# Pooled values of the first batch summed in two chains of transfers and an addition

## The chip, the cores and the metric

The kernel runs on one core of a Trainium2 chip. The metric is the device time of one execution in microseconds. The core's engines take their instructions in program order, each engine from a queue of its own: PE (matmul), DVE (vector), ACT (scalar), POOL, and SP, which here only starts transfers. Engines wait for one another through semaphores; transfers run on 16 shared DMA engines.

## The reference

Attention with two parts that are added, then two feed-forward layers over all 2304 tokens:

```python
# q, k, v: (4 batches, 8 heads, 576 tokens, 64)
q_d, k_d, v_d = mean over groups of 4 tokens          # 144 pooled tokens
out_up = repeat(softmax(q_d k_d^T / 8) v_d, 4)        # each pooled row four times
out_local = softmax(q k^T / 8 where |i - j| < 4) v
x = (out_up + out_local) as (2304, 512)
x = relu(x @ w_in1)**2 @ w_out1                       # w_in1 512x2048, w_out1 2048x512
out = silu(x @ w_in2) @ w_out2                        # a second pair of weights
```

## The kernel before

A list scheduler in Python writes the program. Every step of the work is a coroutine that yields the engine it wants next with an estimated cost; the step that can start earliest by these estimates comes next, and ties are broken by a rank: ten times the place at which it was added, plus an entry of the table SHIFT. What the scheduler decides is fixed when the program is built. On the chip each engine runs its list in order and stalls where its next instruction has to wait.

**Batch 0, the start.** `load_pooled(0)` brings the pooled values of batch 0: the input holds the four members of each group of tokens as four arrays of 72 x 1024 f32 (288 KB), and four transfers issued by POOL (line 412) write the first into the tile `vd_t` (called dst in the traces) and add the other three to it on the way. `pooled(0, hp)`, for the four pairs of heads, sums q and k on DVE (L458) and copies them by PE and ACT (L465, L467), makes scores (L475), the maximum (L479), the exponential (L486), the normalised weights (L492), transposes them (L498, L500) and multiplies them with `vd_t` (L510); ACT takes the result out (L513). The first L510 is the first reader of `vd_t`.

Between these stand eight tiles of 72 tokens of the local attention, `tile_attention(i)`: scores (L586, L589), maximum (L599), exponential (ACT alone, L604, four times, where the tile is in the tuple ATILE; otherwise DVE L608, ACT L611, DVE L614), normalisation on DVE (L268, L616, L617), transposes (L626), copy (L629), product (L638) and copy out (L645). `tiles_done` adds the pooled part to the local one (L890), four head pairs for each half of the batch. `keep_warm` gives PE small products (L1540) where the scheduler expects a gap.

**Weights.** They lie in memory as 8-byte words. `eighth(m, e)` loads 1 MB (SP, L304) into one of three raw buffers and rebuilds 128 x 1024 f32 from it by ACT (L312) and DVE (L268, L271). Here w_in e and w_out e are eighth e of the first pair. They take the buffers in turn (w_in 0, w_out 0, w_in 1, w_out 1, ...), so that a load waits on SP until the eighth three places before it is rebuilt. A later step, `quarter`, squares and sums them (L333, L341, PE L344 and L354).

**The first layer.** The first two chunks of 128 hidden units (L1027, 16 products in two halves of the tokens) need the finished x of batch 0 and w_in 0. The next chunks (L1049, f32) need w_in 1 and so on, the second product is L1106, and from the second stretch of tokens on the products are f16 (L1062, L1106). PE then goes through products with few breaks to the end.

**Batch 1** loads q and k as a whole (SP, L550, L551), sums them on POOL (L432, L434) and goes on to L475. The second pair's w_out is loaded through the tile `gr`, after x2d of the first layer has been read back.

Of the kernel before, what the change touches and what calls it, by code (L numbers as in the profile page):

```python
# [13 lines left out]
ALU = mybir.AluOpType  # L14
# [4 lines left out]
NT, DM, DFF = 2304, 512, 2048  # L19
# [11 lines left out]
HG = NG // 2  # L31
# [10 lines left out]
EXP_MASK = 0x7F800000  # L42
SLACK = 1.02

PADS = (0.4, 0.4, 1.2, 0.4)

ATILE = (0, 2, 3, 4, 5, 14, 15)

FILL = 0.2

SHIFT = {('eighth', 'i2', 0): -185,
 ('eighth', 'i2', 1): -185,
 ('eighth', 'i2', 2): -185,
 ('eighth', 'i2', 3): -185,
 ('eighth', 'i2', 4): -225,
 ('eighth', 'i2', 5): -225,
# [4 lines left out]
 ('load_v', 8): 94,  # L61
 ('load_v', 12): 35,
 ('load_v', 14): 105,
 ('load_v0', 1): -22,
 ('piece', 3, 1, 0): 337,
 ('pooled', 0, 3): 51,
 ('pooled', 3, 3): -81,
 ('products', 10): 1,
 ('quarter', 'i1', 0): -152,
 ('quarter', 'i1', 1): -152,  # L70
 ('quarter', 'i1', 2): -152,
# [3 lines left out]
 ('quarter', 'o1', 3): -77,  # L75
 ('quarter', 'o2', 0): 15,
 ('split_late', 4, 2): 321,
 ('tile_attention', 2): 53,
 ('tile_attention', 3): 72,
 ('tile_attention', 11): 32,  # L80
 ('unit', 8): 52,
 ('unit', 9): -135,
 ('unit', 10): -57}

N1 = 3

# [8 lines left out]
class Schedule:  # L95
# [15 lines left out]
    def mark(self, key):  # L111
        self.events[key] = self.end
# [62 lines left out]
def tile_attention_two_moes(ctx: ExitStack, tc: tile.TileContext, qw, kw, vw, qt, kt, vt, qp, kp, vp, maskd, tmaskd,  # L175
# [7 lines left out]
    V, A, G, PE = nc.vector, nc.scalar, nc.gpsimd, nc.tensor  # L183
# [16 lines left out]
    gr = pool.tile([P, 7 * 512], F32, name="gr")  # L200
# [191 lines left out]
    def raw_buf(at, n=2048):  # L392
        return words(int(at), n).bitcast(U32)
# [4 lines left out]
    vd_t = dst[0:HG, 4 * NGP + 4 * NG:].rearrange("p (c n) -> p c n", c=2)  # L398
# [6 lines left out]
    def load_pooled(b):  # L405
        yield "DVE", 0.1
        V.memset(qd_t[:, :, NG:], 0.0)
        if b == 0:
            for r in range(4):
                yield "POOL", 1.1  # L410
                yield "DMA", 0.82, 2.0
                G.dma_start(out=vd_t, in_=vp[0, r], **({"accum_op": ALU.add} if r else {}))
        else:
            for r in range(4):
                kw_ = {"accum_op": ALU.add} if r else {}
                if b > 1:
                    yield "POOL", 2.1
                    G.dma_start(out=qd_t[:, :, :NG], in_=qp[b - 2, r], **kw_)
                    G.dma_start(out=kd_t, in_=kp[b - 2, r], **kw_)
                yield "POOL", 1.1  # L420
                yield "DMA", 1.5 if b == 1 else 4.5, 2.0
                G.dma_start(out=vd_t, in_=vp[b, r], **kw_)
        outd[b] = p2.tile([P, 4, NG], F32, tag="outd", name="outd")
        mark(("pooled", b))
# [12 lines left out]
    def pooled(b, hp, banks):  # L437
        pad = PADS[b]
        if b > 1:
# [124 lines left out]
    def tile_attention(i, banks):  # L564
# [27 lines left out]
        if i >= 2:  # L592
            yield "event", ("tr", i - 2)
        by_act = i in ATILE
        yield "DVE", 0.48 if by_act else 0.85
# [951 lines left out]
    with tc.manual_schedule():  # L1547
# [40 lines left out]
        for h in range(4):  # L1588
            add(load_qk(0, h))
        add(load_pooled(0))  # L1590
        convert(0)
        for h in range(2):
# [7 lines left out]
        for n in range(1, 16):  # L1600
            convert(n, *([("qk", 0, 3)] if n == 1 else [("at", 3)] if n < 4 else []))
            if n == 3:
                add(split_early(0))
            if n == N1:
                add(load_pooled(1), ("xf", 0))
                for h in range(2):
                    add(load_qk(1, h), ("xf", 0))
                for hp in range(4):
                    add(sums(1, hp), ("xf", 0))
                for hp in range(4):  # L1610
                    add(pooled(1, hp, TWO))
                add(all_pooled(1))
                for i in range(per, 2 * per):
                    add(tile_attention(i, TWO), ("xf", 0))
                add(tiles_done(1))
            if n % 4 == 3 and n >= NFULL:
                add(quarter("i1", n // 4), ("xf", 0))
                add(quarter("o1", n // 4), ("xf", 0))
                add(first_scales(0, 1, n // 4))
# [4 lines left out]
        add(whole("o1"))  # L1624
        add(split_early(1))
        add(load_pooled(2), ("ds", 1), ("at", TPB - 1))
        for hp in range(4):
            add(pooled(2, hp, TWO))
# [14 lines left out]
        r = [[raw_buf(a * 1024)] for a in (22, 26, 28)]  # L1643
# [4 lines left out]
        r = [[gr[:, 1536 + i * 1024:2560 + i * 1024].bitcast(U32) for i in range(2)], [raw_buf(31 * 1024)]]  # L1648
# [122 lines left out]
```

## Time and profile before

| | |
|---|---|
| median of three runs | 882.69 us (879.0, 882.69, 884.89) |
| the profiled execution | 884.28 us, of which the span of the trace is 882.3 |
| PE busy | 851.1 us, 96% of the span |
| DVE, ACT, POOL busy | 673.6, 524.6, 59.7 us |
| granted clock of PE, mean | 0.991 of full speed |

The span runs from the first to the last instruction of the trace; 2.0 us of the execution's time lie outside it. PE is the engine that is nearly always busy, so what counts is where PE waits, or works at a lower clock.

### The profile page before, as it was taken

How to read it: one execution, taken by the hardware profiler on the slowest of the kernel's cores; microseconds unless marked ns; L12 is line 12 of the kernel's file. 1: busy time of each engine (PE TensorE's matmuls, PEld its weight loads, DVE VectorE, ACT ScalarE, POOL GpSimd, SP SyncE). 2: the span in 40 equal slices, each digit the busy share in tenths (PEclk: the TensorE clock that was granted, in tenths of full speed). 3: DMA queues.
4: the chain of work that ended last, by engine and by line, in shares of the span. 5: the costliest groups of instructions: out<-in, count | busy, mean ns of one | idle time of the engine just before them, and what ended most of it. 6: DMA issues, size and time to landing. Idle time of an engine off the chain costs nothing.

```text
span 882.3 us, 14418 instructions
## 1 busy us (share of the span) xinstructions
PE 851.1 (96%) x5578; PEld 507.6 (58%) x5578; DVE 673.6 (76%) x1310; ACT 524.6 (59%) x1026; POOL 59.7 (7%) x86
## 2 busy tenths in 40 slices
PE   8898999999988999999999999999999899999998
PEld 6664554455433444444444445884445778788865
DVE  5567888886667999888988998746988887777731
ACT  3787888888767652435665443666676564344432
POOL 1016113000000400000000000000000110000000
PEclk9899999999999999999999999999999999999999
DMA  9678456844667951242124200322333200010010
GB/s 253 206 200 321 172 157 147 238 164 160 225 201 250 229 135 37 89 155 72 36 84 155 72 28 27 114 61 96 132 113 107 81 25 2 25 49 1 2 48 25
DMA packets 35584, 103.55 MB, mean 117 GB/s; under 512 B 4316, under 2 KB 8540, under 8 KB 32316
## 3 DMA queue, kind: packets, MB, share of 16 engines
q1 hardware_dynamic: 27036, 84.65, 29.0%
q0 software_dynamic: 8192, 17.83, 8.4%
q8 instruction: 44, 0.72, 0.3%
q14 instruction: 24, 0.20, 0.1%
q10 hardware_dynamic: 288, 0.15, 0.1%
HBM read 82.16 MB, written 20.45 MB: 116 GB/s over the span
## 4 chain that ended last, share of the span: by engine, by line
PE 71%; DMA 11%; DVE 8%; ACT 7%; issue 2%; POOL 1%; SPq 0%; POOLq 0%; DVEq 0%; ACTq 0%
PE acc L1106 26%; PE hps L1062 24%; PE seven L1181 6%; PE acc L1216 4%; DMA dst<-vp 4%; DMA wt<-w_in 3%; DMA gr<-w_out 3%; PE hps L1049 2%; DVE ub L1242 1%; DVE gr L271 1%; PE pb L1216 1%; DVE wt L271 1%; ACT sq L333 1%; PE hps L1027 1%; DVE hl L271 1%
## 5 line engine op out<-in xcount | busy, mean ns | idle before, releaser
L1062 PE MATMUL hps<-hl,wt 128*128 128x512 f16 (+1 forms) x1440 | 293.7, 351 | 0.0
L1062 PEld LDWEIGHTS <-wt 128*128 128x128 f16 x1440 | 140.2, 98 | 128.4 <-issue 3.6
L1106 PE MATMUL acc<-gr,wt 128*128 128x512 f16 (+2 forms) x928 | 212.8, 374 | 0.0
L1106 PEld LDWEIGHTS <-wt 128*128 128x128 f16 x864 | 84.5, 99 | 78.3 <-issue 1.2
L271 DVE SCALAR_TENSOR_TENSOR gr<-hps,sc,gr 128x512 f16<-128x512 f32 (+1 forms) x118 | 80.2, 679 | 63.2 <-ACT gr L1476 60.4
L1106 PE MATMUL acc<-wt,gr 128*128 128x512 f16 x480 | 112.0, 379 | 0.1
L1458 ACT ACTIVATE hps<-hps,sc 128x512 f32<-128x512 f32 (+1 forms) x72 | 44.0, 611 | 90.5 <-PE hps L1062 90.2
L1181 PE MATMUL seven<-hl,wt 128*128 128x256 f16 x456 | 80.5, 275 | 5.7 <-DVE ub L1242 5.6
L1473 ACT ACTIVATE hps<-hps,sc 128x512 f32<-128x512 f32 (+1 forms) x46 | 27.4, 596 | 91.5 <-PE hps L1062 87.6
L1106 PEld LDWEIGHTS <-gr 128*128 128x128 f16 x480 | 46.8, 98 | 51.8 <-issue 0.7
L1181 PEld LDWEIGHTS <-wt 128*128 128x128 f16 x672 | 66.1, 98 | 17.9 <-issue 7.5
L1476 ACT ACTIVATE gr<-hps,sc 128x512 f16<-128x512 f32 (+1 forms) x118 | 74.3, 630 | 2.7
L1216 PEld LDWEIGHTS <-gr 128*128 128x128 f16 x672 | 65.6, 98 | 11.0 <-DVE gr L271 2.0
L1216 PE MATMUL acc<-wt,gr 128*128 128x256 f16 x480 | 61.0, 274 | 2.2 <-DVE gr L271 1.1
L1181 PE MATMUL seven<-ub,wt 128*128 128x256 f16 x180 | 49.6, 275 | 0.0
L1242 DVE TENSOR_TENSOR ub<-seven,ub 128x256 f32<-128x256 f32 x74 | 28.6, 419 | 21.8 <-PE seven L1181 20.0
L271 DVE SCALAR_TENSOR_TENSOR wt<-wt,sc 128x1024 f16<-128x1024 f32 x32 | 40.6, 1279 | 4.7 <-ACT wt L372 4.4
L778 DVE TENSOR_REDUCE ub<-ub 128x128 f32<-128x896 f32 x40 | 43.3, 1083 | 1.0
L711 DVE TENSOR_TENSOR ub<-ub,s 128x896 f32<-128x896 f32 x40 | 43.5, 1087 | 0.6
L746 DVE TENSOR_REDUCE s<-ub 128x14 f32<-128x896 f32 x40 | 43.2, 1080 | 0.5
L708 DVE TENSOR_TENSOR ub<-ub 128x896 f32<-128x896 f32 x40 | 43.2, 1081 | 0.0
L271 DVE SCALAR_TENSOR_TENSOR gr<-ub,sc,gr 128x512 f16<-128x512 f32 (+2 forms) x66 | 42.1, 671 | 0.7 <-ACT gr L1476 0.7
(247 smaller groups left out, 1159.1 us busy)
## 6 DMA issues: line engine op xcount, KB each, us to landing
wt<-w_in SPq DMA_DIRECT2D x16, 1024.0 KB, 8.2
wt<-w_out SPq DMA_DIRECT2D x9, 1024.0 KB, 5.5
w<-wt POOLq DMA_DIRECT2D x16, 512.0 KB, 4.6
dst<-w SPq DMA_DIRECT2D x16, 512.0 KB, 3.3
gr<-w_out SPq DMA_DIRECT2D x14, 512.0 KB, 5.4
ub<-vw SPq DMA_DIRECT2D x10, 640.0 KB, 3.8
ub<-kw SPq DMA_DIRECT2D x10, 640.0 KB, 7.2
dst<-vp POOLq DMA_DIRECT2D x16, 288.0 KB, 6.9
```

The costliest lines, as they stand in the source:

```text
L271: V.scalar_tensor_tensor(out=out, in0=in0, scalar=s, in1=in1, op0=op0, op1=op1)
L708: eng.tensor_tensor(out=prod[i % 2].rearrange("p (t w d) -> p t w d", t=2, w=WIN), in0=band(k, j, t0), in1=q[:, j, t0:t0 + 2, :].unsqueeze ...
L711: eng.tensor_tensor(out=prod[i % 2].rearrange("p (t d w) -> p t d w", t=2, d=D), in0=band_v(v, j, t0), in1=prob[u][:, j, t0:t0 + 2, :].uns ...
L746: V.tensor_reduce(out=s[:, j, t0:t0 + 2, :], in_=prod[i % 2].rearrange("p (t w d) -> p t w d", t=2, w=WIN), axis=AX.X, op=ALU.add)
L778: V.tensor_reduce(out=o[:, t0:t0 + 2, j, :], in_=prod[i % 2].rearrange("p (t d w) -> p t d w", t=2, d=D), axis=AX.X, op=ALU.add)
L1062: PE.matmul(out=ps, lhsT=w[:, o:o + P], rhs=x[:, kk, :n], start=(m == 0), stop=(m == 3 * KD - 1))
L1106: PE.matmul(out=a, lhsT=l, rhs=x, start=(first and m == 0), stop=(last and m == len(ops) - 1))
L1181: PE.matmul(out=b7[:, i * 256:(i + 1) * 256], lhsT=a[:, c:c + P], rhs=x, start=(n == 0), stop=(n == 5))
L1216: PE.matmul(out=acc7[p][m][:, t, :], lhsT=a, rhs=b, start=(e == 0 and t == 0 and n == 0), stop=(e == 7 and t == 1 and n == 2))
L1242: V.tensor_tensor(out=out, in0=a, in1=b, op=op)
L1458: A.activation(out=ps, in_=ps, func=AF.Relu, scale=1.0 if exact else cs)
L1476: A.activation(out=gh, in_=ps, func=AF.Copy, scale=sg)
```

## The change

`load_pooled(0)` writes the first and the second array by plain transfers into two tiles, `vd_t` and `vo_t` (a part of `gr`, not in use at that time), adds the third to `vd_t` and the fourth to `vo_t`, and then adds the two tiles by one DVE instruction (L426, 72 x 1024 f32). The scheduler's table of ranks, the tuple ATILE of tiles whose exponential is made by ACT alone, and one entry of PADS (batch 2) are other ones. Line numbers after the change are 11 to 14 higher.

```diff
-PADS = (0.4, 0.4, 1.2, 0.4)
+PADS = (0.4, 0.4, 0.8, 0.4)
-ATILE = (0, 2, 3, 4, 5, 14, 15)
+ATILE = (0, 1, 2, 5, 9, 10, 14, 15)
 SHIFT = {('eighth', 'i2', 0): -185,
...
- ('eighth', 'i2', 2): -185,
...
- ('load_v0', 1): -22,
- ('piece', 3, 1, 0): 337,
+ ('piece', 3, 1, 0): 456,
...
+ ('pooled', 2, 0): -10,
+ ('pooled', 3, 0): 148,
...
+ ('sum_weights', 'o2', 4): 26,
...
- ('unit', 10): -57}
+ ('unit', 10): 108,
+ ('unit', 16): 18}
...
         if b == 0:
-            for r in range(4):
+            vo_t = gr[0:HG, 0:2 * DM].rearrange("p (c n) -> p c n", c=2)
+            for r, t in enumerate((vd_t, vo_t, vd_t, vo_t)):
                 yield "POOL", 1.1
-                yield "DMA", 0.82, 2.0
-                G.dma_start(out=vd_t, in_=vp[0, r], **({"accum_op": ALU.add} if r else {}))
+                yield "DMA", 0.82, 2.0 if r == 3 else 2.0
+                G.dma_start(out=t, in_=vp[0, r], **({"accum_op": ALU.add} if r > 1 else {}))
+            yield "DVE", 1.1
+            V.tensor_tensor(out=vd_t, in0=vd_t, in1=vo_t, op=ALU.add)
```

SP's list at the start, behind the eight loads of q and k of batch 0. First before (L560 loads the values of four tiles, L576 those of one; L304 the weights, w_in and w_out in turn):

```order
L560 DMA wt<-vt 70x4x512
L304 DMA wt<-w_in 128x2048
L560 DMA wt<-vt 70x4x512
L304 DMA wt<-w_out 128x2048
L304 DMA wt<-w_in 128x2048 x2
L304 DMA wt<-w_out 128x2048 x2
L576 DMA wt<-vt 70x512
L304 DMA wt<-w_out 128x2048
L304 DMA wt<-w_in 128x2048 x2
L550 DMA ub<-qt 128x1152
```

and after:

```order
L315 DMA wt<-w_in 128x2048
L574 DMA wt<-vt 70x4x512 x2
L315 DMA wt<-w_out 128x2048
L315 DMA wt<-w_in 128x2048
L315 DMA wt<-w_out 128x2048
L315 DMA wt<-w_in 128x2048
L315 DMA wt<-w_out 128x2048
L315 DMA wt<-w_in 128x2048
L590 DMA wt<-vt 70x512
L315 DMA wt<-w_out 128x2048
L315 DMA wt<-w_in 128x2048 x2
L315 DMA wt<-w_out 128x2048
```

Before, w_in 0, w_out 0, w_in 2, w_in 1, w_out 1 and w_out 3 stand there in this order; after, w_in 0, w_out 0, w_in 2, w_out 3, w_in 1, w_out 1, w_in 5. The load of w_out 3, which waits until w_in 2 is rebuilt, has moved ahead of those of w_in 1 and w_out 1, and the loads of q and k of batch 1 (L550, L564 after) stand further back.

DVE's list around the rebuilding of w_out 0 (the row wt<-wt of L268 and that of L271), before:

```order
L479 TENSOR_REDUCE dmx<-acc_369 128x3
L268 TENSOR_SCALAR dmx<-dmx 128x3
L268 TENSOR_SCALAR wt<-wt 128x1024
L271 SCALAR_TENSOR_TENSOR wt<-wt 128x1024
L268 TENSOR_SCALAR asm<-asm 128x4
L616 RECIPROCAL asm<-asm 128x4
L617 TENSOR_TENSOR ae<-ae,asm 128x280
L268 TENSOR_SCALAR dsm<-dsm 128x3
L491 RECIPROCAL dsm<-dsm 128x3
L492 TENSOR_TENSOR hl_71<-hl_71,dsm 128x432
```

and after (L279 and L282 are the L268 and L271 of before):

```order
L493 TENSOR_REDUCE dmx<-acc_391 128x3
L279 TENSOR_SCALAR dmx<-dmx 128x3
L279 TENSOR_SCALAR wt<-wt 128x1024
L628 TENSOR_REDUCE asm<-ae 128x4
L279 TENSOR_SCALAR asm<-asm 128x4
L630 RECIPROCAL asm<-asm 128x4
L631 TENSOR_TENSOR ae<-ae,asm 128x280
L282 SCALAR_TENSOR_TENSOR wt<-wt 128x1024
L426 TENSOR_TENSOR dst<-dst,gr 72x1024
L279 TENSOR_SCALAR dsm<-dsm 128x3
L505 RECIPROCAL dsm<-dsm 128x3
```

The four rows of a tile of the local attention (L628 to L631) have come between the two rows that rebuild w_out 0, and behind them stands the new addition, ahead of everything else that DVE has to do.

ACT's list at the end of batch 0's attention (L629 is the copy before the last product of a tile, L645 the copy out, L312 a rebuilding of weights), before:

```order
L645 ACTIVATE wt<-acc_613 128x4x64
L611 ACTIVATE ae<-ae 128x280
L645 ACTIVATE wt<-pa 128x4x64
L629 ACTIVATE hl_70<-pa 70x512
L629 ACTIVATE hl_70<-pb 70x512
L645 ACTIVATE wt<-pa 128x4x64
L645 ACTIVATE wt<-pb 128x4x64
L312 ACTIVATE wt<-wt 128x1024
```

and after (L643, L659 and L323 are the same three):

```order
L643 ACTIVATE hl_70<-pa 70x512
L643 ACTIVATE hl_70<-acc_640 70x512
L625 ACTIVATE ae<-ae 128x280
L659 ACTIVATE wt<-pa 128x4x64
L659 ACTIVATE wt<-pb 128x4x64
L323 ACTIVATE wt<-wt 128x1024
L643 ACTIVATE hl_70<-pa 70x512
L659 ACTIVATE wt<-pa 128x4x64
L323 ACTIVATE wt<-wt 128x1024
L669 ACTIVATE sq,sc<-wt 128x256 x2
```

The rebuilding of w_out 3 (the first L323) has come ahead of the copy of the last tile, tile 7, which the last products of batch 0's attention and then the first layer wait for. On PE, one group of scores and one set of transposes more stand ahead of the first L510, and seven of the 16 products of L1027 stand ahead of the last tile's product, where two of their 32 passes stood before.

## Rows read from the trace of the kernel before

**Rows 1.** Page, part 4: the chain that ended last, by engine and line

```profile
PE 71%; DMA 11%; DVE 8%; ACT 7%; issue 2%; POOL 1%; SPq 0%; POOLq 0%; DVEq 0%; ACTq 0%
PE acc L1106 26%; PE hps L1062 24%; PE seven L1181 6%; PE acc L1216 4%; DMA dst<-vp 4%; DMA wt<-w_in 3%; DMA gr<-w_out 3%; PE hps L1049 2%; DVE ub L1242 1%; DVE gr L271 1%; PE pb L1216 1%; DVE wt L271 1%; ACT sq L333 1%; PE hps L1027 1%; DVE hl L271 1%
```

**Rows 2.** Timeline of POOL: start us, us, what [idle before <-releaser]

```profile
1.47 0.75 POOL L412 DMA_DIRECT2D dst<-vp  x1 [0.16 <-issue]
8.84 0.85 POOL L412 DMA_DIRECT2D dst<-vp  x1 [6.62 <-DMA dst<-vp]
20.83 0.82 POOL L412 DMA_DIRECT2D dst<-vp  x1 [11.14 <-DMA dst<-vp]
27.79 1.15 POOL L412 DMA_DIRECT2D dst<-vp  x1 [6.14 <-DMA dst<-vp]
```

**Rows 3.** Timeline of PE, 0 to 60

```profile
30.77 0.22 PE L586 MATMUL acc<-tmask,ident_b 64*64 64x70 bf16 x2
...
31.61 0.28 PE L1540 MATMUL warm<-ones_w,ones_b 128*128 128x256 bf16 x1
33.66 0.71 PE L510 MATMUL pb<-wt,dst 72*64 72x144 f32 x8 [1.77 <-DMA dst<-vp]
...
36.12 0.86 PE L498 MATMUL pb<-ident,hl 128*72 128x128 f32 x3
36.77 1.91 PE L626 MATMUL acc<-ident,ae 128*70 128x128 f32 x8
...
50.81 6.74 PE L1027 MATMUL hps<-wt 128*128 128x256 f32 x30
57.40 2.84 PE L1049 MATMUL hps<-wt 128*128 128x512 f32 x6
```

**Rows 4.** Windows: busy of each engine, PEclk, DMA share, GB/s

```profile
10.00:20.00 10.00, 9.84 (x132) 7.99 (x127) 7.11 (x22) 4.79 (x24) 0.00 (x0) 1.00 1.03 267
...
34.00:41.00 7.00, 7.00 (x65) 5.42 (x60) 0.47 (x3) 3.65 (x15) 0.00 (x0) 0.52 0.91 371
```

**Rows 5.** Timeline of ACT, 0 to 60

```profile
20.91 1.13 ACT L312 ACTIVATE wt<-wt 128x1024 f32<-128x1024 f32 x1 [1.56 <-DMA wt<-w_in]
...
25.89 0.38 ACT L645 ACTIVATE wt<-pa 128x256 f32<-128x256 f32 x1 [0.45 <-PE pa L638]
26.94 1.13 ACT L312 ACTIVATE wt<-wt 128x1024 f32<-128x1024 f32 x1 [0.67 <-DMA wt<-w_out]
...
43.25 1.15 ACT L312 ACTIVATE wt<-wt 128x1024 f32<-128x1024 f32 x1
...
49.06 0.59 ACT L629 ACTIVATE hl<-pb 70x512 f32<-70x512 f32 x1 [0.64 <-PE pb L626]
```

**Rows 6.** Timeline of DVE, 0 to 60

```profile
28.10 0.76 DVE L268 TENSOR_SCALAR wt<-wt 128x1024 uint32<-128x1024 uint32 x1 [0.51 <-ACT wt L312]
...
48.25 1.42 DVE L890 TENSOR_TENSOR wt<-wt,outd 128x256 f32<-128x256 f32 x4
...
50.31 1.23 DVE L271 SCALAR_TENSOR_TENSOR wt<-wt 128x1024 uint32<-128x1024 uint32 x1
```

**Rows 7.** Page, part 5: busy us, mean ns of one, idle before

```profile
L271 DVE SCALAR_TENSOR_TENSOR wt<-wt,sc 128x1024 f16<-128x1024 f32 x32 | 40.6, 1279 | 4.7 <-ACT wt L372 4.4
...
L711 DVE TENSOR_TENSOR ub<-ub,s 128x896 f32<-128x896 f32 x40 | 43.5, 1087 | 0.6
```

**Rows 8.** Timeline of SP, 0 to 60; line L304's transfers to landing

```profile
30.19 1.26 SPq L304 DMA_DIRECT2D wt<-w_in  x2
31.56 20.38 SPq L304 DMA_DIRECT2D wt<-w_out  x2
...
DMA to landing us min/median/max: 4.8/5.8/10.8
```

**Rows 9.** Waits of PE: us in total, times, longest

```profile
PE pa L354 <- ACT sq L333: 5.5, 2, 3.0
...
PE pa L354 <- DVE ae L608: 2.0, 1, 2.0
```

More of the change, by code (lines that the diff above doesn't have):

```diff
@@ L63 @@
  ('load_v', 14): 105,
- ('load_v0', 1): -22,
- ('piece', 3, 1, 0): 337,
+ ('piece', 3, 1, 0): 456,
+ ('piece', 3, 1, 1): 110,
+ ('piece', 3, 1, 2): 110,
+ ('piece', 3, 1, 3): 110,
+ ('piece', 4, 2, 2): 32,
+ ('piece', 9, 4, 1): 10,
+ ('piece7', 8, 3): -22,
  ('pooled', 0, 3): 51,
+ ('pooled', 2, 0): -10,
+ ('pooled', 3, 0): 148,
  ('pooled', 3, 3): -81,
  ('products', 10): 1,
+ ('products', 15): 5,
  ('quarter', 'i1', 0): -152,
@@ L77 @@
  ('split_late', 4, 2): 321,
+ ('split_late', 7, 2): 10,
+ ('sum_weights', 'i2', 7): -4,
+ ('sum_weights', 'o2', 4): 26,
  ('tile_attention', 2): 53,
```

## The prediction

> **What bounds the kernel now.** I read the shares first: PE is busy for 96% of the span, and the chain that ended last runs over PE for 71% and over transfers for 11%, of which 4% is one thing, dst<-vp [rows 1]. So almost everywhere only PE's own work counts, and a change of order can win only where PE waits or runs slowly. The places that this change touches come next. On POOL's timeline the four transfers of batch 0's pooled values stand in one row, each issued only when the one before has landed: 7.1, 11.7 and 6.7 us from issue to landing (from row to row, less 0.3 us to issue the next), and the last takes 5.8 to 33.6, when PE's first L510 starts [rows 2, 3]. PE's timeline shows the price: a last small product at 31.61 that ends at 31.89, then 1.77 us of waiting for that transfer [rows 3]. The windows show a second one: from 34 to 41 the granted clock is 0.52, that is the lower of the two levels (1.2 against 2.4 GHz), while PE is busy for all 7.0 us [rows 4]. The stage ends with 6.7 us of L1027 and the first L1049 at 57.40 [rows 3]. I take that time, the first L1049, as the measure of the whole start: behind it PE goes on nearly without gaps.
>
> **The change part by part.** All sums stand against the profiled execution, 884.28 us (span 882.3 and 2.0 outside it), which is 1.6 above the median of 882.69; the differences are then applied to the median.
>
> *The transfers.* The first two now start together and the third waits only for the first. Even if each took as long as the slowest of the four, 11.7 us, two in a row would have landed at 1.5 + 23.4 + 0.6 = 25.5 [rows 2]; I expect 21 to 25.5, instead of 33.6. The landing so ends nothing any more. What is late next is DVE, in whose list the addition stands behind the second row of the rebuilding of w_out 0, and into this rebuilding the normalisation of a tile has been put.
>
> *When the addition runs.* ACT rebuilds w_out 0 (its part) behind more work than before. It starts with w_in 0, which before was taken up at 20.91 when it landed [rows 5] and whose load now stands one place earlier on SP, ahead of 560 KB of values: I take 20.3. Up to w_out 0 stand in ACT's new list one such rebuilding (1.05 from start to start), two groups of four L604 (1.18 each), three L486, five L500, an L467, two L629, two L645: 8.1 us by the durations of the same instructions in the trace, and two waits for PE like the 0.45 ahead of L645 [rows 5]: 9.0 in all, so 29.3 instead of 26.94. Then 1.13 on ACT, 0.76 for DVE's first row [rows 5, 6], 1.3 for the tile's four small rows, 1.23 for the second: 33.7. The addition itself is not in the trace. Its neighbours are L711, 128x896 in 1.09 us, and L271, 128x1024 in 1.28 [rows 7]; as 72 partitions with 1024 elements each are nearest to the latter in length, I take 1.2. So the values are ready at 34.9, 1.2 us later than before. The bounds: 33.3, where PE itself arrives (31.89 and the 1.4 us of work which now stand ahead of L510, below), and 35.9 with a landing of w_in 0 a microsecond later. Behind the addition on DVE stand the weights of the last pair of heads and a tile's maximum; they are read by PE behind the L510s and come in time. **Term A: +1.2 us** (-0.4 to +2.2).
>
> The trace speaks of the transfers' sharing first: from 10 to 20 us, where the 11.7 us transfer lies, the DMA engines are full (1.03, 267 GB/s) [rows 4], so two at once there don't run twice as fast. The Trainium skill, "DMA: Bandwidth & Descriptors", section "Issuing engines are not separate DMA queues", says the same in a stronger form: all transfers run on the same 16 engines and interleave, and starting them together saves only the time of starting. By that rule the two chains would take as long as the four in a row, and the time would be 879 to 881 (the third rival, below); the trace agrees with it for the full stretch alone. The rows show 6.7 and 5.8 us for 288 KB [rows 2], which at 371 GB/s [rows 4] would be 0.8, so most of each is not bandwidth and can overlap.
>
> *The end of the stage.* One group of scores (30.77 to 31.61, 0.84 us) and one set of transposes (0.6) stand now ahead of L510, where PE waits anyway, and seven of the 16 L1027 ahead of the last tile's product, of which before only one stood there: 6 x 0.44 us = 2.6 (30 passes take 6.74 [rows 3], two make a product). These 1.4 + 2.6 us come off the tail if nothing else holds it: **term B: -4.0 us**.
>
> *What holds it.* On ACT, the rebuilding of w_out 3 stands ahead of the copy of tile 7. Its load waits on SP until w_in 2 is rebuilt, in a place where before only w_out 3 itself and what followed waited: the second L304 of w_out sits there to 51.94 [rows 8]. Now w_in 1 and w_out 1 are queued behind it. ACT came to w_in 2 at 43.25 before, 9.6 us behind the first L510 [rows 3, 5]. In the new lists there stand between them on PE three L510 (2.5 us, 33.66 to 36.12), one L498 (0.7), one L638 (0.7) and one L626 (0.9, half of the x8), at the halved clock [rows 3], then a copy of 0.6 on ACT: 34.9 + 5.4 = 40.3, and 3.1 us for ACT and DVE: 43.4. The load lands 4.8 to 10.8 us after its issue, 5.8 in the median [rows 8]; I take 5.8 and, three loads starting together, 8.3 as its far end: 49.2. Then 1.15 for ACT [rows 5], 0.59 for the copy, 0.7 for L638, 0.38 for L645, 0.36 for one L890 (four take 1.42 [rows 6]) and eight L1027 at 0.44: 6.7. The first L1049 starts at **55.9**, against 57.40 + 1.2 - 4.0 = 54.6 without this wait; so **term C: +1.3** (0 to +3.8). w_in 1, which this L1049 reads, lands some 2.8 us behind w_out 3 (1 MB at the 371 GB/s of a full stretch [rows 4]) and is rebuilt 3.1 us later: 55.1, just in time.
>
> A + B + C is -1.5 at the first L1049.
>
> *Later.* PE waits 5.5 us in two places for ACT's squares of the second w_out (L354) [rows 9]. The end of the f32 stretch from which that chain of loads starts comes 12 products earlier in PE's new order, and the sums 3 earlier: 9 x 0.216 us more time for the loads. **Term D: -1.9** (0 to -5.5). The loads of batch 1's q and k, whose sums on POOL an L475 of PE needs, have moved back on SP behind more weights, by 2.8 us for each megabyte at the 371 GB/s above; but in PE's new order eight f32 products more stand ahead of that L475, 0.9 us each (two passes, six in 2.84 [rows 3]). Near this place PE also waits 2.0 us for DVE once (L354 [rows 9]), which may go. **Term E: 0** (-2.0 to +2.8). The other ranks move pieces of an f16 stretch in which PE doesn't wait; costed at 0, covered by PE's own work, with ±2 if a piece comes late once or a wait goes.
>
> Sum: -1.5 - 1.9 = -3.4. 884.28 becomes 880.9, the median 882.69 **879.3**.
>
> **The rivals.** *Faster.* If the addition is done by 33.3, PE has no gap ahead of L510, and the clock need not fall. Then L510 starts 0.4 earlier, and the 7 us at 0.52 shrink by 3.4 [rows 4]. The rebuilding of w_in 2 ends at 38.4 instead of 43.4 (1.6 and 3.4 earlier), and with 5.8 and 6.7 us behind it the first L1049 would start at 50.9, -6.5; with D 8.4 us less: **874.3**. For it speaks that 8.1 us of ACT's work without any wait would have the addition done at 34.0; against it that 0.7 us are even then still missing, and that ACT waits in every such stretch of the trace.
>
> *Slower.* The order of the three loads. If w_in 2 is rebuilt as late as before (50.31 + 1.23 = 51.5 [rows 6]), since something ahead of it on ACT or DVE waits, then w_out 3 lands at 57.3, and w_in 1 and w_out 1 behind it, which in the trace had been issued at 30.19 to 31.56 and lay ready [rows 8]. The first L1049 would start at 64.0: +6.6 - 1.9 = +4.7, **887.4**. It decides from the point where this rebuilding ends later than 46.8 (46.8 + 12.5 - 57.4 = 1.9). For it speaks that in this list SP, ACT and PE wait for each other in a ring; against it, that the tail ahead of that step became shorter.
>
> *Not what it says.* The two chains take as long as the four did, and the fourth lands at 33.6 or later. The addition can't begin sooner than 33.7 in any case, so the time is the forecast's, or up to 2 us more: **879 to 881**.
>
> **How the numbers follow.** Forecast 0.57 (879.3, with its bounds 873 to 885), faster rival 0.18 (874.3), slower rival 0.17 (887.4), no overlap 0.08. The range reaches over both rivals' times: 873 to 888.5. About 1%, 8.8 us, is what a measurement of this kernel can tell from no change (its three runs lie 5.9 apart). Faster than 873.9: somewhat under half of the faster rival and the end of the forecast in which D takes all of 5.5, together 0.11. Slower than 891.5: a quarter of the slower rival and a little, 0.05. Within: 0.84.
>
> **What would show it.** The four vp transfers: the last landed by 25.5, DVE's addition at 33.7 for 1.2 us, and PE's wait ahead of the first L510 ended by DVE instead of a transfer, near 34.9. A halved clock in the 7 us behind it. ACT's L323 ahead of tile 7's copy waiting for w_out, and the first L1063 near 55.9. L365 waiting for 3.6 us in all instead of 5.5. The prediction is wrong if the gap ahead of L510 is gone together with the halved clock (faster), if w_out 3 lands after 53 (slower), or if a new wait of more than 3 us stands anywhere behind 60 us, of which nothing in the rows speaks.

## The result, and the profile after

| | before | after |
|---|---|---|
| median of 13 runs each | 879.5 us (875.28 to 888.73) | 884.38 us (879.49 to 890.14) |
| ratio, 95% interval | | 1.0053 [1.003, 1.0076]: slower |
| the profiled execution, its span | 884.28, 882.3 | 890.14, 888.4 |
| PE busy, mean granted clock | 851.1, 0.991 | 857.5, 0.985 |

The forecast was 879.3 against 882.69, a gain of 0.4%; the kernel became 0.5% slower. Both profiled executions lie on the long side of their kernels' runs, so the 6.0 us between them are compared by place first, and sizes are then taken from the ratios of many runs.

To find the place I set the starts of the large products of both kernels (lines L1027, L1049, L1062, L1106, L1181, L1216 and those that answer to them after) side by side in their order and took the difference of the n-th ones. After the change the first L1063 stands 0.7 us later than the L1049 of before; at 293 and 306 us the difference is 0.9; at 320 (times of the kernel before) it is 7.0; at the end 6.0. Between 60 and 293 us it swings from -8 to +6 us, and around 420 up to 14, where the two lists place other work at different points between these products. So in this pair of executions nearly all of the loss arises within 14 us, in the second layer, some 280 us behind the start that the change is about.

First the start. POOL's timeline after the change, which answers to [rows 2] (start us, us, what, idle before and releaser):

```profile
1.48 0.75 POOL L424 DMA_DIRECT2D dst<-vp  x1 [0.17 <-issue]
2.22 0.55 POOL L424 DMA_DIRECT2D gr<-vp  x1
8.85 0.87 POOL L424 DMA_DIRECT2D dst<-vp  x1 [6.08 <-DMA dst<-vp]
10.71 0.84 POOL L424 DMA_DIRECT2D gr<-vp  x1 [1.00 <-DMA gr<-vp]
```

The two chains do overlap: the two later transfers are issued at 8.85 and 10.71, so the values are at hand some 12 us sooner than before (b_pool, below, starts to add them at 20.8; before, the last landed at 33.6). ACT's timeline, which answers to [rows 5] (L323 rebuilds weights):

```profile
18.66 1.14 ACT L323 ACTIVATE wt<-wt 128x1024 f32<-128x1024 f32 x1 [1.05 <-DMA wt<-w_in]
...
28.99 1.12 ACT L323 ACTIVATE wt<-wt 128x1024 f32<-128x1024 f32 x1 [2.04 <-DMA wt<-w_out]
...
49.81 1.15 ACT L323 ACTIVATE wt<-wt 128x1024 f32<-128x1024 f32 x1
50.85 0.59 ACT L643 ACTIVATE hl<-pa 70x512 f32<-70x512 f32 x1
```

DVE's, which answers to [rows 6], with the addition (L426):

```profile
32.01 1.22 DVE L282 SCALAR_TENSOR_TENSOR wt<-wt 128x1024 uint32<-128x1024 uint32 x1
33.14 1.21 DVE L426 TENSOR_TENSOR dst<-dst,gr 72x1024 f32<-72x1024 f32 x1
```

And PE's timeline, which answers to [rows 3]:

```profile
31.57 0.78 PE L640 MATMUL acc<-ident,ae 128*70 128x128 f32 x4 [2.10 <-ACT hl L500]
...
34.86 1.23 PE L524 MATMUL pb<-wt,dst 72*64 72x144 f32 x8
...
50.65 1.89 PE L1041 MATMUL hps<-wt 128*128 128x256 f32 x8
52.47 0.69 PE L652 MATMUL pa<-hl,wt 70*64 70x64 f32 x16
...
54.10 3.72 PE L1041 MATMUL hps<-wt 128*128 128x256 f32 x16 [0.32 <-DVE wt L904]
58.08 3.70 PE L1063 MATMUL hps<-wt 128*128 128x512 f32 x8 [0.26 <-ACT gr L1477]
```

The first product with the pooled values (L524) starts at 34.86, and the wait for vp is gone. DVE has the sum ready at 34.35, but PE is busy with other products until it comes to L524, so here the addition doesn't set its start. What held PE up stands earlier: ACT now waits 2.04 us for the load of w_out 0; what is behind it in ACT's list (L500) comes late, and PE waits 2.10 us for that at 29.5. From 31.9 to 42.1 the clock is granted at half. The windows of the kernel after show it in a row that answers to the second of [rows 4] (the third number from its end is the granted clock):

```profile
31.00:42.00 11.00, 10.38 (x86) 8.22 (x87) 7.50 (x19) 4.51 (x14) 0.00 (x0) 0.54 0.28 98
```

0.54 is nearly the lower of the two levels, 1.2 of 2.4 GHz.

Now the place of the loss. SP's timeline after the change, from 300 us on:

```profile
303.85 0.33 SPq L746 DMA_DIRECT2D ub<-qw  x1
304.24 0.44 SPq L747 DMA_DIRECT2D ub<-kw  x1
304.77 12.04 SPq L976 DMA_DIRECT2D xi<-x2d  x3
```

ACT's timeline in the same kernel and stretch:

```profile
307.93 0.67 ACT L1490 ACTIVATE gr<-hps,sc 128x512 f16<-128x512 f32 x1
314.96 0.72 ACT L889 ACTIVATE hl<-xi,sc 128x512 f16<-128x512 f32 x1 [6.36 <-issue]
316.12 0.72 ACT L889 ACTIVATE hl<-xi,sc 128x512 f16<-128x512 f32 x1 [0.44 <-DMA xi<-x2d]
316.86 1.28 ACT L1487 ACT_TABLE_LOAD   x1
318.15 0.66 ACT L1487 ACTIVATE hps<-hps,sc 128x512 f32<-128x512 f32 x1
318.74 0.68 ACT L1517 ACTIVATE gr<-acc,sc 128x512 f32<-128x512 f32 x1
```

And PE's:

```profile
313.50 2.75 PE L1076 MATMUL hps<-hl,wt 128*128 128x512 f16 x12
319.47 5.28 PE L1120 MATMUL acc<-wt,gr 128*128 128x512 f16 x12 [3.21 <-ACT gr L1517]
```

In the windows, the granted clock behind the wait (again the third number from the end):

```profile
320.00:325.00 5.00, 5.00 (x14) 1.65 (x12) 4.09 (x11) 4.79 (x7) 0.00 (x0) 0.50 0.60 213
```

The same stretch of SP's timeline in the kernel before:

```profile
297.33 0.86 SPq L962 DMA_DIRECT2D xi<-x2d  x2
303.84 0.33 SPq L732 DMA_DIRECT2D ub<-qw  x1
```

ACT's timeline there, with the scaling (L875 before):

```profile
307.57 1.32 ACT L875 ACTIVATE hl<-xi,sc 128x512 f16<-128x512 f32 x2
```

And PE's, which has no wait:

```profile
315.17 3.00 PE L1106 MATMUL acc<-wt,gr 128*128 128x512 f16 x12
```

Here xi<-x2d (L962 before, L976 after) reads a piece of the first layer's output back for the second layer's second stretch of tokens, and ACT's L889 scales it. qw and kw are the loads of unit 11 of the local softmax work in batch 3; they wait on SP for a buffer that DVE frees at 303.8, in both kernels. Before, the two loads of xi stood ahead of them and started at 297.3; after, they stand behind and start at 304.8. They land about 10 us later, the DMA engines being full (share 1.08 to 1.12 from 305 to 320), and ACT, which meets L889 in its list at 308.6, stands until 315. The profile names no releaser for this first row ("issue"); that it is the load follows from the second row, which names it, and from a_xi below, where the loads come some 6 us earlier and this wait is gone. Behind L889 stand the instructions that empty PE's accumulators (L1517) and make its next operands (L1487, L1490). PE waits 3.21 us, and then the clock is granted at half (0.50) for 6.8 us, from 318.6: twelve products take 5.28 us instead of 2.75.

### The profile page after: what moved, and what is told of

The parts are those of the page before. It is cut to its first block, busy times and chain, and to the rows that moved or that the text cites. A ratio compares the mean times of both kernels' runs of the same rounds, so it can differ in the third digit from the quotient of the medians.

```text
span 888.4 us, 14411 instructions
## 1 busy us (share of the span) xinstructions
PE 857.5 (97%) x5577; PEld 509.8 (57%) x5577; DVE 674.2 (76%) x1310; ACT 525.7 (59%) x1033; POOL 62.5 (7%) x86
## 4 chain that ended last, share of the span: by engine, by line
PE 68%; DVE 13%; DMA 10%; ACT 6%; issue 2%; SPq 0%; ACTq 0%
PE acc L1120 26%; PE hps L1076 25%; PE seven L1195 7%; PE acc L1230 4%; DMA wt<-w_in 4%; DVE wt L282 2%; DMA gr<-w_out 2%; DMA wt<-w_out 2%; DVE gr L282 2%; DVE ub L1256 1%; DMA xi<-x2d 1%; ACT wt L323 1%; PE pb L1230 1%; DMA ub<-kt 1%; DVE wt L279 1%
## 5 line engine op out<-in xcount | busy, mean ns | idle before, releaser
L282 DVE SCALAR_TENSOR_TENSOR gr<-hps,sc,gr 128x512 f16<-128x512 f32 (+1 forms) x118 | 80.2, 679 | 64.8 <-ACT gr L1490 62.1
L1120 PE MATMUL acc<-wt,gr 128*128 128x512 f16 x480 | 114.8, 385 | 3.2 <-ACT gr L1517 3.2
L1487 ACT ACTIVATE hps<-hps,sc 128x512 f32<-128x512 f32 (+1 forms) x46 | 27.4, 596 | 85.7 <-PE hps L1076 85.6
L1490 ACT ACTIVATE gr<-hps,sc 128x512 f16<-128x512 f32 (+1 forms) x118 | 74.4, 631 | 2.7
L282 DVE SCALAR_TENSOR_TENSOR wt<-wt,sc 128x1024 f16<-128x1024 f32 x32 | 40.8, 1280 | 4.5 <-ACT wt L383 4.3
L279 DVE TENSOR_SCALAR wt<-wt 128x1024 uint32<-128x1024 uint32 (+1 forms) x39 | 24.1, 619 | 26.4 <-ACT wt L323 26.1
L725 DVE TENSOR_TENSOR ub<-ub,s 128x896 f32<-128x896 f32 x40 | 43.4, 1085 | 0.5
```

Of the source, the lines that this page charges most:

```text
L282: V.scalar_tensor_tensor(out=out, in0=in0, scalar=s, in1=in1, op0=op0, op1=op1)
L725: eng.tensor_tensor(out=prod[i % 2].rearrange("p (t d w) -> p t d w", t=2, d=D), in0=band_v(v, j, t0), in1=prob[u][:, j, t0:t0 + 2, :].uns ...
L1120: PE.matmul(out=a, lhsT=l, rhs=x, start=(first and m == 0), stop=(last and m == len(ops) - 1))
L1490: A.activation(out=gh, in_=ps, func=AF.Copy, scale=sg)
```

## The experiments

All were timed in turns with the kernel before on the same chip (12 executions each, b_two 6). Theory 1: the loss is this wait, made by the place of the loads of xi. Rival: the loss is at the start (the lower clock there, or transfers that take bandwidth from the weights), and the wait at 316 us is made good later.

**a_xi.** The kernel after, in which unit 11's loads wait in the scheduler until both loads of xi have been issued. At 300 us SP then has them ahead of unit 11's, as before; PE's list is not touched.

```diff
+        if u == 11:
+            yield "event", ("asked", 3, 1)
+            yield "event", ("asked", 3, 0)
...
+            mark(("asked", p, i))
```

> The changed kernel with two transfers (the first two loads of x2d for the second layer's second stretch) put back ahead of the local unit's loads of q and k on SP; PE's list is the same. Theory 1: the loss comes from these two loads standing behind a load that waits for VectorE, which makes ScalarE and then PE wait 3.2 us at 316 us and halves the clock behind it; then the wait and the halved stretch go, and the time falls by 5 to 6 us, to 0 to 1.5 us above the kernel before in the profile's count (ratio to before 0.998 to 1.002). Rival: the loss comes from the start (the later w_out and the longer halved clock); then the time stays where it is (ratio 1.004 to 1.007).

Measured: 881.51 against 880.19, 1.0009 [0.9981, 1.0037]. SP's timeline in its trace:

```profile
294.63 0.85 SPq L979 DMA_DIRECT2D xi<-x2d  x2
300.07 0.33 SPq L749 DMA_DIRECT2D ub<-qw  x1
```

ACT's timeline, where L892 is the scaling:

```profile
304.71 1.32 ACT L892 ACTIVATE hl<-xi,sc 128x512 f16<-128x512 f32 x2
```

PE's timeline, at the place of the wait:

```profile
314.90 2.75 PE L1080 MATMUL hps<-hl,wt 128*128 128x512 f16 x12
317.49 2.75 PE L1124 MATMUL acc<-wt,gr 128*128 128x512 f16 x12
```

The scaling waits for nothing, and PE goes through. By the medians more than three quarters of the loss are gone (0.53% to 0.09%). Theory 1 holds so far.

**b_xi.** The reverse edit in the kernel before: the loads of xi wait until unit 11's are issued.

```diff
+        mark(("asked", u))
...
+        if p == 3:
+            yield "event", ("asked", 11)
```

> The kernel before with the same two loads put behind the local unit's loads of q and k on SP, and nothing else of the change. Theory 1: the wait of about 3 us for ScalarE near 316 us appears with a halved clock behind it, and the time rises by 5 to 6 us (ratio 1.005 to 1.007). Rival (the start causes the loss): no change (0.998 to 1.002).

Measured: 878.96 against 880.19, 0.9992 [0.9965, 1.0019]. The expectation missed. The loads do stand behind, but PE doesn't wait. SP's timeline:

```profile
298.73 1.01 SPq L965 DMA_DIRECT2D xi<-x2d  x2
```

ACT's timeline:

```profile
304.00 0.66 ACT L1476 ACTIVATE hps<-hps,sc 128x512 f32<-128x512 f32 x1 [1.22 <-PE hps L1065]
304.65 0.69 ACT L1506 ACTIVATE gr<-acc,sc 128x512 f32<-128x512 f32 x1
305.24 0.68 ACT L1479 ACTIVATE gr<-hps,sc 128x512 f16<-128x512 f32 x1
308.03 0.72 ACT L876 ACTIVATE hl<-xi,sc 128x512 f16<-128x512 f32 x1 [2.12 <-DVE s L747]
309.05 0.72 ACT L876 ACTIVATE hl<-xi,sc 128x512 f16<-128x512 f32 x1 [0.30 <-DMA xi<-x2d]
```

The miss says more than a hit would have: the scheduler, told of the later load, also set ACT's scaling (L876) behind the three instructions that PE waits for. So a late load alone cost nothing here; to cost time it would have to meet an ACT list in which its reader stands first. I call this theory 1a.

**a_est** tests 1a. The loads of xi stay behind qw and kw, and only the scheduler's estimate of their landing goes from 2.0 to 3.5 us, which moves the scaling on ACT behind L1487, L1517 and L1490.

```diff
-        yield "DMA", 0.7, 2.0
+        yield "DMA", 0.7, 3.5 if p == 3 and i < 2 else 2.0
```

> The changed kernel with the two loads of x2d left behind the local unit's loads on SP, but ScalarE's list with the output step of the running products (L1487, L1517, L1490) ahead of the scaling of the loaded x (L889) instead of behind it; PE's list is the same. Theory 1a: what costs time at 316 us is ScalarE's list, where the scaling that waits for the late load blocks the steps that PE waits for; then the loads land as late as now (some 10 us after their issue), PE waits under 0.7 us there, and the time falls by 4 to 5 us, as in the run with the loads put back (ratio to before 0.998 to 1.003). Theory 1b: the late loads themselves hold PE (the next stretch's x comes late): the wait stays, at another place, and so does the time (1.004 to 1.007).

Measured: 880.78 against 880.37, 1.0012 [0.9991, 1.0034]. SP's timeline:

```profile
300.74 0.33 SPq L746 DMA_DIRECT2D ub<-qw  x1
301.13 0.51 SPq L747 DMA_DIRECT2D ub<-kw  x1
301.73 0.94 SPq L976 DMA_DIRECT2D xi<-x2d  x2
```

ACT's timeline:

```profile
308.66 0.69 ACT L1517 ACTIVATE gr<-acc,sc 128x512 f32<-128x512 f32 x1
309.24 0.68 ACT L1490 ACTIVATE gr<-hps,sc 128x512 f16<-128x512 f32 x1
311.42 0.72 ACT L889 ACTIVATE hl<-xi,sc 128x512 f16<-128x512 f32 x1 [1.50 <-DVE s L760]
312.63 0.72 ACT L889 ACTIVATE hl<-xi,sc 128x512 f16<-128x512 f32 x1 [0.49 <-DMA xi<-x2d]
```

PE's timeline, at the products that waited in the kernel after:

```profile
312.99 2.75 PE L1120 MATMUL acc<-wt,gr 128*128 128x512 f16 x12
```

The loads take about as long as in the kernel after, 9.7 us from the issue to the first scaling and 10.9 to the second (10.2 and 11.4 there), and PE doesn't wait. Two different edits take the ratio from 1.0053 to 1.0009 and 1.0012. In the traces both leave PE's and POOL's lists as they are, and those of SP, ACT and DVE differ from the kernel after's only between 294 and 337 us. a_est's start has the wait ahead of L640 (1.85 us) and a lower clock from 31.9 for 10.2 us, just as in the kernel after, so the start is not what the edit repaired.

**a_warm** turns to the start: 18 small products more on PE (they enter no result), ahead of tile 3's transposes, to keep the clock up. **b_warm** does the same in the kernel before, 15 of them ahead of the first L510.

```diff
+    def more_warm(n):
+        for _ in range(n):
+            PE.matmul(out=warm_t[0], lhsT=ones_b, rhs=ones_w, start=True, stop=True)
...
+        if i == 3:
+            more_warm(18)
```

> The changed kernel with 18 small products more on PE ahead of the transposes of tile 3, where PE waits 2.1 us for ScalarE; nothing else moves. If that wait is what lowers the granted clock from 31.9 to 42.1 us, the stretch stays at full clock, the first L510 is no earlier (VectorE's addition sets it, 34.9), and the first chunk of the first layer starts 2 to 4 us earlier than 58.1; time 2 to 4 us less. Rival: the clock falls for the light work before it in any case, or the loads hold the stage: first chunk within 0.5 us, time the same.

> The kernel before with 15 small products more on PE ahead of the first L510, where PE waits 1.5 to 1.8 us for the chain of four transfers; nothing else moves. If the wait is what lowers the clock there (34.3 to 41.2 us), that stretch stays at full clock and the time falls by 1 to 3 us (ratio 0.996 to 0.999). Rival: the clock falls in any case or is given back at the next wait: 0.999 to 1.002.

Measured: a_warm 885.22 against 880.19, 1.006 [1.0034, 1.0086]; b_warm 879.59 against 879.02, 1.0005 [0.9978, 1.0033]. In both traces the clock at the start stays at full speed, and both times are those of their kernels without the products, so the gains of 2 to 4 and 1 to 3 us that were expected missed. In a_warm the wait of the second layer still stands, 2.6 us. How far the products themselves keep the clock up these two traces can't tell: a_xi and a_late, without them, have it at full speed from 31 to 42 us as well. So no gain from the start's clock is shown, and a_warm loses as much as the kernel after.

**a_late** puts 14 clears of an unused part of gr on POOL between the first two transfers and the last two, which start at 16.8 and 17.3 instead of 8.85 and 10.71.

```diff
+                if r == 2:
+                    for _ in range(14):
+                        G.memset(gr[:, 2048:3072], 0.0)
```

> The changed kernel with POOL held up for some 10 us (14 clears of unused memory) between the first two and the last two transfers of pooled values; no other list changes. If the transfers running two at a time delay w_out 0 (ScalarE waits 2.0 us for it, to 28.99), it is taken up at 26.9 to 27.3, PE's wait of 2.1 us ahead of tile 3's transposes goes to under 0.5, the first L510 comes at 32 to 33.5 instead of 34.9, and the first chunk of the first layer 1 to 4 us earlier. Rival: w_out 0 is late for its place on SP (issued at 10.5 instead of 8.8) and not for the transfers: it lands as late as now, and nothing moves, or the later transfers themselves hold the addition.

Measured: 882.86 against 880.19, 1.0028 [1.0003, 1.0054]. ACT waits 0.58 us for w_out 0 instead of 2.04, and the first product of the first layer's f32 stretch comes 2.5 us earlier than in the trace of before; the wait of the second layer is there again, 3.21 us. But w_out 0 is taken up at 28.32 and not at 26.9 to 27.3, and a_xi, whose program at the start is the kernel after's without any clears, shows the same: a wait of 0.75 us, w_out 0 at 28.31, that product at 55.28 (54.89 here). So this start lies within what one execution differs from the next, and the trace doesn't show that the clears did it. Whether the 0.25% to the kernel after are more than chance can't be told from overlapping intervals.

The next four part the change itself. **b_pool** is the kernel before with nothing but the two chains; POOL adds the two tiles, so that every other list stays as it was. **b_two** is before's table of ranks with the new `load_pooled`, DVE adding, so that the scheduler orders all anew by the old ranks. **a_four** is the reverse: the new ranks with the chain of four.

```diff
-            for r in range(4):
+            vo_t = gr[0:HG, 0:2 * DM].rearrange("p (c n) -> p c n", c=2)
+            for r, t in enumerate((vd_t, vo_t, vd_t, vo_t)):
...
-                G.dma_start(out=vd_t, in_=vp[0, r], **({"accum_op": ALU.add} if r else {}))
+                G.dma_start(out=t, in_=vp[0, r], **({"accum_op": ALU.add} if r > 1 else {}))
+            G.tensor_tensor(out=vd_t, in0=vd_t, in1=vo_t, op=ALU.add)
```

> The kernel before with the two chains of transfers alone: the addition is made by POOL, and every other engine's list and all ranks are those of before. If the chain of four transfers is what the start waits for, PE's wait of 1.5 to 1.8 us ahead of the first L510 goes, the halved clock behind it is shorter or gone, and the first chunk of the first layer starts 1.5 to 4 us earlier: ratio 0.995 to 0.998. Rival: two transfers at a time delay w_out 0 by 1.5 to 3 us and ScalarE's list behind it, and PE waits for that instead: ratio 0.999 to 1.002.

> The changed way of loading (two chains and VectorE's addition) with the ranks, the tuple of tiles and the pads of before; the scheduler sets the order anew. If the loss comes from the new ranks' order near 316 us alone, this kernel, in whose SP list the loads of x2d stand ahead of the local unit's, has no wait there and lies at 0.996 to 1.003. If the two chains themselves cost time, 1.003 or more.

> The new ranks with the chain of four transfers of before; the scheduler sets the order anew. SP's list has the loads of x2d ahead of the local unit's again. By the theory that the loss is the order at 316 us: no wait there, ratio 0.997 to 1.003, with PE's wait for the transfers ahead of the first L510 (1.5 to 1.8 us) back. Rival (the new ranks cost time in several places): above 1.004.

Measured: b_pool 884.49, 1.0058 [1.0036, 1.008]; b_two 893.04, 1.0153 [1.012, 1.0186]; a_four 884.05, 1.0053 [1.003, 1.0076], all against 880.37. POOL's timeline in b_pool:

```profile
20.78 2.42 POOL L414 TENSOR_TENSOR dst<-dst,gr 72x1024 f32<-72x1024 f32 x1 [9.01 <-DMA gr<-vp]
```

ACT's timeline there:

```profile
24.36 1.12 ACT L312 ACTIVATE wt<-wt 128x1024 f32<-128x1024 f32 x1 [3.80 <-DMA wt<-w_in]
```

PE's:

```profile
26.13 0.86 PE L500 MATMUL acc<-ident,wt 128*72 128x128 f32 x3 [2.88 <-ACT wt L502]
...
37.71 0.71 PE L512 MATMUL pb<-wt,dst 72*64 72x144 f32 x8
```

The sum is ready at 23.2, 10 us sooner, and yet the product that reads it (L512 here) comes 4.05 us later than before: w_in 0 is now taken up at 24.36 instead of 20.91 (19.72 and 21.54 in b_xi and b_warm, whose start up to there is the same program as before's), ACT waits for it 3.80 instead of 1.56 us, and PE for ACT. The time lies above both ranges that were expected, and it is w_in 0 that is late, not w_out 0 as the rival had it. b_two shows the same more strongly (ACT waits 6.42 us for w_in 0, to 25.82; PE 5.5 us behind it); at the place in the second layer PE waits 0.6 us at most, and the time lies where its expectation put a cost of the two chains. But the scheduler has set other orders too: side by side with before's profiled execution b_two's is 4.3 us behind at 60 us and 6.6 at the end, its median is 12.7 us longer, and where the rest arises is not explained. The windows tell why w_in 0 is late: from 12 to 20 us the DMA engines are full in both kernels (shares of 1.05 and 1.01), at 252 GB/s in b_pool and 255 in before. No more bytes come in there by starting two chains; what the pooled values gain, w_in 0 loses. In the kernel after, with another order of loads (280 GB/s there, at a share of 0.99), w_in 0's load has moved one place forward on SP and is taken up at 18.66, and it is w_out 0 that is late.

In a_four PE doesn't wait at 316 us (its two loads of xi stand ahead of qw, and ACT scales both at 302.0 without waiting for them), and still it is as slow as the kernel after; the expectation missed, and the time is the one that its rival named (costs in several places). Its profiled execution, with waits of 1.6 us at 72.6 and 1.9 at 589.6, ends 2.2 us ahead of the profiled one of before, and is the shortest of its 12 runs, so the trace doesn't show what its median lost. I leave that open: the new ranks alone (a_four) and the two chains alone (b_pool) each cost some half a per cent, and both together without the wait (a_xi, a_est) 0.1%.

**b_stag** and **ax_stag** try to keep the good part: the first three arrays go through one chain as before, and only the fourth is loaded beside the third, into the second tile. b_stag does it in the kernel before with POOL's addition, ax_stag in a_xi with DVE's.

```diff
-            for r, t in enumerate((vd_t, vo_t, vd_t, vo_t)):
+            for r, t in enumerate((vd_t, vd_t, vd_t, vo_t)):
...
-                G.dma_start(out=t, in_=vp[0, r], **({"accum_op": ALU.add} if r > 1 else {}))
+                G.dma_start(out=t, in_=vp[0, r], **({"accum_op": ALU.add} if r in (1, 2) else {}))
```

> The kernel before with the first three transfers in one chain as before and only the fourth to a second tile, beside the third; POOL adds the two tiles. All other lists are those of before. In the first 20 us no byte moves earlier than before. If the two chains cost time only because they take the memory's bandwidth from w_in 0 early, w_in 0 is taken up at 19.5 to 21 again, the pooled values are ready at 28 to 31, PE's wait of 1.5 to 1.8 us ahead of the first L510 goes, and the time falls by 1.5 to 4 us (ratio 0.995 to 0.999). Rival: what cost time was POOL's addition (2.4 us, holding up VectorE beside it) or the second tile itself: ratio above 1.002.

> The changed kernel with the loads of x2d put back ahead of the local unit's, and its four transfers as three in a chain and one beside the third; VectorE's addition stays where it is. If early bandwidth is what makes w_out 0 late (28.3 to 29 us), it is taken up by 27.5, the first L510 comes before 33, and the time is 1 to 3 us below the same kernel with two full chains (ratio to before 0.997 to 1.000). Rival: w_out 0 is late for its place on SP, and the time is that of the kernel with two full chains (1.001).

Measured: b_stag 881.77, 1.0029 [0.9996, 1.0062]; ax_stag 878.7, 0.9994 [0.9968, 1.0019], both against 879.02. b_stag's gain missed, and its interval leaves open whether its rival (a cost of POOL's addition) holds; ax_stag's time fits both sides of its expectation, and its places missed (w_out 0 by 27.5, the first L510 before 33). In b_stag POOL's addition at 30.13 holds DVE's rebuilding beside it (below), and the first L512 starts at 33.58 without a wait, no sooner than before's 33.66 with one. In ax_stag w_in 0 is taken up at 17.43, yet ACT waits 3.73 us for w_out 0, to 29.77, with one transfer of values at a time until 18.0 us, and the first L524 comes at 35.93. So the early pair is shown to delay w_in 0 (b_pool, b_two); that it is what delays w_out 0 in the kernel after is not shown. a_four, which has the chain of four and up to 30 us the same lists as the kernel after on SP, ACT, DVE and PE, takes w_out 0 up at 25.72, against 28.15 to 29.06 in after, a_xi, a_est and a_warm; but before, b_xi and b_warm, one program up to there, take it up anywhere from 25.11 to 28.29, so that one trace doesn't settle it. No version was found that is shown to beat the kernel before.

## Why the prediction was wrong

**The step that failed** is "The other ranks move pieces of an f16 stretch in which PE doesn't wait; costed at 0, covered by PE's own work, with ±2". The piece is the pair of loads of xi, moved behind unit 11's on SP, and PE's own work could not cover it: ACT takes its list in order, and the scaling of these loads stood ahead of what PE needs next. Neither the new ranks alone (a_four) nor the new loading alone (b_two) makes this order; in both traces the loads of xi stand ahead of qw. In the three traces of kernels that have it (after, a_warm, a_late) the wait is 3.2, 2.6 and 3.2 us, and with the lower clock that follows it the place costs 6.1, 4.2 and 4.8 us by the side-by-side starts of the products at 306 and 320 us. By the ratios it costs 0.0053 - 0.0009 = 0.44% or 0.0053 - 0.0012 = 0.41%, 3.9 or 3.6 us of 879.5; by the intervals of these ratios that is uncertain by some 3 us either way (an estimate), but clear of 0. The forecast had named such a wait, over 3 us behind 60 us, as what would make it wrong. The place could have been read beforehand: in the trace of before these loads start only 6.5 us ahead of qw, qw waits for DVE, and another load of xi is waited for by ACT for 3.04 us at 315 already. I had not compared SP's order in that stretch.

**Term A** (+1.2, to 34.9) was met to the tenth, 34.86, by chance, since the way was another. ACT came to w_out 0 at 26.95, not 29.3: w_in 0 was taken up 1.6 us earlier than I had it, and the 9.0 us from there took 8.3. It then waited 2.04 us for the load, which I had taken to be there. The addition cost 1.21 (1.2 taken) and ended at 34.35, not 34.9; L524 did not wait for it, as was forecast, but stood behind PE's own work, PE having lost 2.10 us ahead of L640, for ACT, and worked at half its clock after that. In the other traces of kernels with these lists, L524 starts at 33.7 to 33.9 (a_xi, a_late, a_est: 33.74, 33.77, 33.88), in the first two after a wait of 0.4 us for the addition.

**Terms B and C** (-4.0 and +1.3, the first L1049 at 55.9): the rebuilding of w_in 2 ends at 44.5 (43.4 taken) and that of w_out 3 starts at 49.81 without waiting (49.2 taken). Behind it 8.3 us pass instead of 6.7, mostly because tile 7's product (L652), whose operand ACT has ready at 51.44, waits 1.0 us on PE behind eight passes of L1041, and because the last 16 passes take 3.7 instead of 3.5 us and the first L1063 waits 0.3 for ACT: 58.08. In a_xi, a_late, a_est and a_warm it is 55.3, 54.9, 56.9 and 56.6. But the kernel before has this spread too, 57.40 in the profile and 54.0 in b_xi, whose start is the same program. So a gain of 1.5 us can't be told here from what one execution differs from the next, and a single profile could not have shown it.

**Term D** (-1.9): the L354 of before waits 5.5 us for ACT's squares, the L365 of after 4.3; but b_xi, with before's order there, shows 4.3 as well. No gain is shown. **Term E**: the 2.0 us wait for DVE went, and one of 1.2 came elsewhere; but in b_xi, with before's order, it is 0.5 us, so it belongs to one execution more than to the order. 0 is not contradicted.

**The rivals.** The faster one (no gap ahead of L510 and no lower clock) didn't happen in the profiled execution, where the clock fell; where it did not fall (a_xi, a_late) the time did not come near 874 either. The slower one (three loads in a ring) didn't happen: w_out 3 lay ready. The third, that the two chains take as long as four in a row, did not either: the last two are issued by 11 us. But the reason given for it is what b_pool shows. Its rule, the Trainium skill, "DMA: Bandwidth & Descriptors", section "Issuing engines are not separate DMA queues" (transfers started by any engine run on the same 16 engines and interleave), agrees with the 252 and 255 GB/s above; I had asked only what it does to the chain and not who else is on those engines. The prediction's estimate of 0.8 us of bandwidth for 288 KB left out that w_in 0 pays: in b_pool it is taken up 2.8 to 4.6 us later than in the three traces with before's start.

In sum: -3.4 forecast; +0.8 and +1.1 of everything but the wait by a_xi and a_est (0.09 and 0.12%, intervals from -0.2 to +0.4%), and 3.6 to 3.9 for the wait at 316 us. So even without the wait the forecast's gain (a ratio of 0.996) lies outside both intervals. Terms B and D were sized as gains and show none; whether the start, D or another place lost it stays open.

## What to carry to other kernels

When a table of ranks is found anew, compare every queue's order through the whole program, and look above all for a load that has moved behind a waiting one and whose reader stands early in the list of an engine that PE depends on; an estimate that is too short by a few microseconds decides such places (2.0 to 3.5 us here, worth 0.4%). A chain of transfers that was split in two while the DMA engines were full took its gain from another load (b_pool, b_two): ask who lands later. A start that differs by 3.4 us from one execution to the next can't be judged by one profile.

## What the runs showed of the hardware

**POOL's addition and DVE beside it.** 72x1024 f32 took DVE 1.21 us and POOL 2.42 (b_pool) and 2.63 (b_stag). While POOL added, some rows of DVE stood. DVE's timeline in b_stag:

```profile
30.60 3.25 DVE L271 SCALAR_TENSOR_TENSOR wt<-wt 128x1024 uint32<-128x1024 uint32 x1
```

and in b_pool:

```profile
20.91 0.44 DVE L616 TENSOR_REDUCE asm<-ae 128x4 f32<-128x280 f32 x1
21.39 1.84 DVE L268 TENSOR_SCALAR asm<-asm 128x4 f32<-128x4 f32 x1
```

L271 and L268 take 1.23 and 0.17 us otherwise, and end 1.09 and 0.03 us after POOL does (32.76 and 23.20). The L616 ahead, a reduction of one input, ran beside POOL's addition in its usual 0.44 us. The Trainium skill, "SBUF — State Buffer", section "SBUF: two separate sides", says that the two engines share a pair of ports as an exclusive lock, so that the later one stands until the first is done; L271 agrees (POOL's end and then nearly its whole 1.23). The section names operations of DVE with two inputs in this memory or in a mode that uses both ports; whether L268, a small 128x4 operation, is in that mode the trace doesn't tell, but it stood as well.

**The landing of a load.** Between the issue of the two loads of xi and ACT's first scaling lie 9.3 to 10.2 us in five traces (after, a_est, a_warm, a_late, b_xi), each with the DMA engines full (shares of 1.10 to 1.12 over that stretch), where the program's own estimate was 2.7. In all five the second scaling is then held 0.3 to 0.5 us more by its own load.
